# Banded attention and MLP on one core: edge and global products over all 128 rows, global attention of two pairs transposed together

## The chip, the cores and the metric

The kernel runs on one core of one Trainium2 chip. The metric is the device time of one execution in microseconds (us). For the kernel before it is 1170.29 us, the median of 3 runs (1169.29 to 1170.46). A difference of 0.2%, about 2.3 us, is what a measurement of this kernel can tell from no change.

## The reference, cut to what matters

There are 8 batches, 8 heads of 64 elements, 512 local and 32 global tokens. Global queries attend to all 544 keys; a local query attends to the 32 global keys and to local keys at most 32 positions away. The result goes through an MLP with gelu.

```python
s_g = scale * q_g @ k_all.T                 # k_all = [k_g, k_l]
out_g = softmax(s_g) @ v_all
s_ll = where(abs(i - j) <= 32, scale * q_l @ k_l.T, -1e9)
s_lg = scale * q_l @ k_g.T
out_l = softmax([s_lg, s_ll]) @ [v_g, v_l]
x = concat([out_g, out_l], axis=2)          # (4352, 512) after a reshape
out = gelu(x @ w_in) @ w_out                # 512 -> 2048 -> 512
```

## The kernel before

**Arithmetic.** All large products run in float32r. An operand is kept as a rounded part (hi) and the rest (lo), and a product is three products (hi hi, hi lo, lo hi) that are summed in PSUM. The splitting is done by ScalarE (ACT), VectorE (DVE) and GpSimd (POOL): one copies hi, another subtracts to get lo.

**Units and chunks.** Attention goes by units (batch, half of its 512 local queries, pair of heads), 64 in all. The MLP goes by chunks of 256 tokens, 16 of them and a last one for the global queries of all batches. While the MLP of one half batch is on TensorE (PE), the attention steps of the next half batch's four units stand between its products. The order of all steps comes from a table of numbers (`PRM`) and a list of due times; PE's instructions are held to this order, and the other engines' orders are made by the scheduler of the tile framework.

**A unit.** `st_s` multiplies queries and keys (tiles `s`; 12 products over 64 rows, since a head has 64 elements; the two heads of a pair lie on different rows of PE). `st_m` (DVE) adds the mask and takes the maximum, `st_e` (ACT) the exponential, `st_n` the normalization (tile `ge` holds the gathered edge columns), `st_t` transposes the result on PE (tile `t`), `st_ah` and `st_al` split it into hi and lo (tile `at`). `st_v` splits the values: `raw` (tile `vr`) comes by DMA, `vs` gets hi (copy) and lo (POOL subtraction, L530). `st_o` (L705 to L720) multiplies for one head j: four products into PSUM tile `o`. The first three run over all 128 rows. The fourth, for the edge keys of the tile next to an end of the sequence, runs over 64 rows: both heads share slot 6 of `vs`, head 0 in partitions 0 to 63 and head 1 in 64 to 127 (L713, L717). `st_c` and `st_x` add the halves of `o`.

**Global queries.** `st_sg` gives the scores of the 32 global queries (tile `sg`), gathered in `sgr`: rows are (pair, head, query), so one `sgr` holds two pairs, a group g. There are 16 groups. `gu_min`, `gu_exp`, `gu_norm` make the softmax. Then, pair by pair (i = 0, 1): `gu_t` (L783 to L791) transposes 64 rows of `sgr` in five pieces, four of 128 keys and one of the 32 global keys (tile `gt`, pool `ps_s`); `gu_a` splits into `agt`; `gu_o` (L817 to L824) multiplies in five products, the last over 32 rows (tile `go`); `gu_s`, `gu_x`, `gu_y` add the parts and transpose the result back (`gos`, `gx`, `gc`, `xg`). `agt` is one buffer, so `gu_a` of pair 1 waits until `gu_o` of pair 0 has read it.

**MLP.** `ml_h` makes h (L865 to L867), `ml_g` the gelu on ACT, `ml_l` its splitting (`gh`, and `gl` on POOL at L386), `ml_o` the second product (`acc`, L889 to L891), `ml_e` copies the result to `ob` and sends it out.

**Pools.** In PSUM, `ps_s` has two buffers for `s`, `sg`, `gt`, `go` and `gx`, and `ps_t` has two for `t` and `o`. In SBUF, the tag `vr` has two buffers for the raw values and `ob`.

**Weights.** At the start the weights come in 32 blocks as 64-bit numbers and are turned into float32 hi and lo by DVE, ACT and POOL (`w_1` to `w_4`, tiles `wraw`, `wi`, `wo`); `late_tiles` then puts `xg`, `vgs` and `agt` in their place.

Of the kernel before, what the change touches and what calls it, by code (L numbers as in the profile page):

```python
# [8 lines left out]
F32 = mybir.dt.float32  # L9
# [30 lines left out]
# Places of the steps in the order of the program, relative to their plain  # L40
# places, and (E_) the engines of steps that several engines can do.
# [282 lines left out]
def attn_mlp(ctx, tc, q_l, k_l, v_l, q_g, k_g, v_g, w_in, w_out, out):  # L324
# [29 lines left out]
    for half in range(2):  # L354
        m = cp.tile([P, WS + WF], BF16, name=f"mask{half}")
        nc.gpsimd.memset(m, 0.0)
        # (column, first key block's distance in keys from the tile's first
        # query, width) of the local key runs of the windows
# [98 lines left out]
    vs = cp.tile([P, 7, 2, D], F32R, name="vs")  # L457
# [4 lines left out]
    sgr = [cp.tile([P, R], F32, name=f"sgr{j}") for j in range(2)]  # L462
    gs = cp.tile([P, NP, P], F32R, name="gs")
# [3 lines left out]
    def late_tiles():  # L467
        # in the place of the weights' raw words
        wx.close()
        lp = ctx.enter_context(tc.tile_pool(name="lp", bufs=1))  # L470
        late["xg"] = lp.tile([P, NP, CH], F32, name="xg")
        late["vgs"] = lp.tile([P, 10, 2, D], F32R, name="vgs")
        late["agt"] = lp.tile([P, 5, 2, 2, SG], F32R, name="agt")

    # Blocks of 32 tokens x 32 elements of a pair of heads, for the transposes
    # of blocks: partitions are (head, half of the elements, token).
# [25 lines left out]
    # Values: slots are (tile 0, head 0), (tile 0, head 1), (tile 1, ...), the  # L502
    # full tile's edge rows for head 0 and 1, the simple tile's edge rows with
    # head 0 in the lower and head 1 in the upper partitions.
    def load_v(u):
        b, half, p = u
        raw = ap_.tile([P, 7, D], F32, name="vr", tag="vr", bufs=2)
# [15 lines left out]
        for r0, src, s0 in es:  # L523
            for j in range(2):
                nc.sync.dma_start(out=raw[64 * j + r0:64 * j + r0 + 32, 6, :], in_=src[j, s0:s0 + 32, :])
# [6 lines left out]
    def st_v(u):  # L532
        split_v((u,), vs, 7)

    # Exponentials and gelus stay in the order in which they are written here:
    # each change between them is a load of ScalarE's tables.
# [38 lines left out]
    def st_tg(b):  # L575
        # columns of a pair's scores for the globals: (hi, lo), head, query
# [8 lines left out]
    def windows(half):  # L585
        # (first key column, width, query tile) of the simple and the full tile
# [4 lines left out]
    # both heads at once (j = 0): the heads of a pair are on different rows of the tensor engine  # L591
# [17 lines left out]
    # columns of the simple and the full tile's windows; 224:256 stays zero  # L609
# [95 lines left out]
    def st_o(u, j):  # L705
# [7 lines left out]
        er = slice(64 * j, 64 * j + 64)  # L713
# [3 lines left out]
              (vs[er, 6], at0[er, :, 3, :], qs)]  # L717
# [4 lines left out]
    # o holds [V hi; V lo] x [A hi | A lo]  # L722
# [60 lines left out]
    def gu_t(g, i):  # L783
        # transposes of one pair's rows: [key, (head, query)]
        s = sgr[g[1]]
        r = slice(64 * i, 64 * i + 64)
# [307 lines left out]
```

## Time and profile before

| what | value |
|---|---|
| median of 3 runs | 1170.29 us |
| span of the profiled execution (first to last instruction) | 1168.5 us |
| PE busy | 1072.6 us, 92% |
| PE's weight loads (PEld) busy | 931.0 us, 80% |
| DVE busy | 775.4 us, 66% |
| ACT busy | 648.8 us, 56% |
| POOL busy | 444.2 us, 38% |
| granted PE clock, mean | 0.992 |

The profiled execution has no time of its own beside its span; the span stands 1.8 us below the median of the runs. PE's products are pipelined, so a product's duration is longer than the step from its start to the next one's start; what a product costs PE is read from such steps. A row of the timeline has the start, the time from there to the end of the row's last instruction, the engine, the line, the operation with its tiles, rows*columns of the array that it uses, partitions x elements of what it reads, and how many instructions were merged (x4). What stands in brackets is the time for which the engine sat idle before it and what ended that.

### The profile page before, as it was taken

Reading aid. Unit: us, or ns where it says so; the run is one execution under the profiler, and the core shown is the slowest. Engines: PE = TensorE matmul, PEld = TensorE weight load, DVE = VectorE, ACT = ScalarE, POOL = GpSimd, SP = SyncE. Lnnn points to the kernel's source line nnn. Section 1 sums busy time; section 2 is a strip of 40 time slices with the busy share of each in tenths; the row PEclk is TensorE's granted clock in tenths of the full one; section 3 lists DMA queues with packets and bytes.
Section 4 is the critical chain, followed back from the end, with each engine's and each line's share of the span. In section 5 each row is a group of like instructions: output and inputs, shape, how many; then the busy total and the mean of one; then the engine's idle time right before and its main releaser. Section 6 shows DMA issues by size and latency. Waiting matters only on the chain.

```text
span 1168.5 us, 21956 instructions
## 1 busy us (share of the span) xinstructions
PE 1072.6 (92%) x7104; PEld 931.0 (80%) x7104; DVE 775.4 (66%) x2281; ACT 648.8 (56%) x1566; POOL 444.2 (38%) x418
## 2 busy tenths in 40 slices
PE   0354789999999999999999999999999999999998
PEld 0234678888888888888888888888888888888996
DVE  7999997677756676567756776667656776653000
ACT  2454567456555665566656665566556655664222
POOL 5434545333433344334333433333433433343221
PEclk9999889999999999999999999999999999999999
DMA  7355423213221232123221322133212322121000
GB/s 210 99 139 137 114 72 77 41 27 77 55 64 26 64 66 57 33 55 67 63 45 41 63 53 64 21 77 61 55 30 64 65 54 41 42 49 32 1 19 19
DMA packets 283123, 71.21 MB, mean 61 GB/s; under 512 B 268417, under 2 KB 276609, under 8 KB 283009
## 3 DMA queue, kind: packets, MB, share of 16 engines
q1 hardware_dynamic: 272256, 53.04, 22.0%
q10 hardware_dynamic: 10752, 16.78, 4.7%
q8 instruction: 56, 0.92, 0.3%
q14 instruction: 59, 0.48, 0.1%
HBM read 60.82 MB, written 8.91 MB: 60 GB/s over the span
## 4 chain that ended last, share of the span: by engine, by line
PE 77%; DVE 10%; DMA 3%; issue 3%; ACT 3%; SPq 2%; POOL 1%; ACTq 0%; DVEq 0%; POOLq 0%
PE h L865 11%; PE acc L889 10%; PE h L867 10%; PE h L866 10%; PE acc L891 9%; PE acc L890 9%; PE o L719 7%; PE s L605 3%; PE go L823 2%; PE t L688 2%; DMA wraw<-in_moe_w_in_dram 2%; DVE wraw L434 1%; DVE a_t L624 1%; PE sg L747 1%; DVE wraw L433 1%
## 5 line engine op out<-in xcount | busy, mean ns | idle before, releaser
L386 POOL TENSOR_TENSOR gl<-gf,gh 128x512 fp32r<-128x512 f32 x136 | 180.5, 1327 | 360.7 <-ACT gh L379 197.3
L865 PE MATMUL h<-xh,wi 128*128 128x256 f32 x1088 | 316.6, 291 | 0.0
L866 PE MATMUL h<-xl,wi 128*128 128x256 f32 x1088 | 305.8, 281 | 0.0
L867 PE MATMUL h<-xh,wi 128*128 128x256 f32 x1088 | 305.5, 281 | 0.0
L889 PE MATMUL acc<-wo,gh 128*128 128x512 f32 x544 | 225.7, 415 | 0.4 <-DVE gh L381 0.4
L865 PEld LDWEIGHTS h<-xh,wi 128*128 128x128 f32 x1088 | 205.7, 189 | 15.3 <-issue 0.6
L891 PE MATMUL acc<-wo,gh 128*128 128x512 f32 x544 | 214.8, 395 | 0.0
L890 PE MATMUL acc<-wo,gl 128*128 128x512 f32 x544 | 212.8, 391 | 0.8 <-POOL gl L386 0.8
L866 PEld LDWEIGHTS h<-xl,wi 128*128 128x128 f32 x1088 | 206.2, 190 | 6.0
L867 PEld LDWEIGHTS h<-xh,wi 128*128 128x128 f32 x1088 | 205.9, 189 | 0.0
L540 ACT ACTIVATE gf<-h 128x512 f32<-128x512 f32 x136 | 81.4, 598 | 165.4 <-PE h L867 156.2
L530 POOL TENSOR_TENSOR vs<-vr,vs 128x448 fp32r<-128x448 f32 x64 | 75.5, 1179 | 236.2 <-DVE vs L381 133.3
L540 ACT ACTIVATE a_t<-a_t,sm 128x192 f32<-128x192 f32 (+1 forms) x256 | 116.9, 458 | 56.3 <-DVE sm L630 55.9
L540 ACT ACT_TABLE_LOAD x91 | 116.8, 1283 | 47.3 <-PE h L867 45.8
L702 DVE TENSOR_TENSOR at<-t,at 128x512 fp32r<-128x512 f32 (+1 forms) x128 | 74.8, 618 | 83.4 <-ACT at L379 83.0
L719 PE MATMUL o<-at,vs 128*128 128x256 f32 (+1 forms) x512 | 115.5, 331 | 6.9 <-DVE at L702 6.9
L891 PEld LDWEIGHTS acc<-wo,gh 128*128 128x128 f32 x544 | 102.3, 188 | 24.3
L605 PE MATMUL s<-k,q 64*128 64x192 f32 (+1 forms) x768 | 70.2, 300 | 55.2 <-ACT vs L379 27.5
L889 PEld LDWEIGHTS acc<-wo,gh 128*128 128x128 f32 x544 | 102.3, 188 | 19.5 <-DVE gh L381 0.5
L890 PEld LDWEIGHTS acc<-wo,gl 128*128 128x128 f32 x544 | 102.9, 189 | 13.5 <-POOL gl L386 1.4
L719 PEld LDWEIGHTS o<-at,vs 128*128 128x128 f32 (+1 forms) x512 | 83.0, 197 | 35.1 <-DVE at L702 7.1
L605 PEld LDWEIGHTS s<-k,q 64*128 64x128 f32 x768 | 56.2, 201 | 62.6 <-ACT vs L379 27.5
(89 smaller groups left out, 1707.1 us busy)
## 6 DMA issues: line engine op xcount, KB each, us to landing
kraw<-in_k_l_dram SPq DMA_DIRECT2D x256, 36.0 KB, 2.0
wraw<-in_moe_w_in_dram ACTq DMA_DIRECT2D x16, 512.0 KB, 4.4
wraw<-in_moe_w_out_dram ACTq DMA_DIRECT2D x16, 512.0 KB, 4.0
qraw<-in_q_l_dram SPq DMA_DIRECT2D x256, 32.0 KB, 1.9
vr<-in_v_l_dram SPq DMA_DIRECT2D x128, 64.0 KB, 2.1
vr<-in_v_l_dram SPq DMA_DIRECT2D x64, 128.0 KB, 2.4
out_dram<-ob SPq DMA_DIRECT2D x32, 256.0 KB, 2.1
vr<-in_v_g_dram SPq DMA_DIRECT2D x192, 16.0 KB, 1.9
```

What stands on the lines that cost most here:

```text
L386: (nc.vector if e == "v" else nc.gpsimd).tensor_sub(**kw)
L530: nc.gpsimd.tensor_sub(out=t[:, :n, 1, :], in0=raw[:, :n], in1=t.bitcast(F32)[:, :n, 0, :])
L540: x = nc.scalar.activation(func=func, **kw).ins
L605: nc.tensor.matmul(out=st[u, "s", jj][:, c:c + w], lhsT=qq[pr, qt * P:qt * P + P], rhs=kk[pr, k0:k0 + w], start=(i == 0 and n == 0), stop= ...
L702: nc.vector.tensor_sub(out=at[:, 1], in0=st.pop((u, "t", j))[:, :n * P].rearrange("p (n q) -> p n q", q=P), in1=at.bitcast(F32)[:, 0])
L719: nc.tensor.matmul(out=o[:, :, qsl], lhsT=l.rearrange("p s e -> p (s e)"), rhs=r, start=(n == 0), stop=(n == 3), skip_group_check=True)
L865: nc.tensor.matmul(out=h, lhsT=hi, rhs=xh[:, c], start=(c == 0), stop=False, skip_group_check=True)
L866: nc.tensor.matmul(out=h, lhsT=hi, rhs=xl[:, c], start=False, stop=False, skip_group_check=True)
L867: nc.tensor.matmul(out=h, lhsT=lo, rhs=xh[:, c], start=False, stop=(c == NCC - 1), skip_group_check=True)
L889: nc.tensor.matmul(out=acc[t], lhsT=gh[:, f % 2, tsl], rhs=hi, start=(f == 0), stop=False)
L890: nc.tensor.matmul(out=acc[t], lhsT=gl[:, f % 2, tsl], rhs=hi, start=False, stop=False)
L891: nc.tensor.matmul(out=acc[t], lhsT=gh[:, f % 2, tsl], rhs=lo, start=False, stop=(f == NF - 1))
```

## The change

**Edge products.** `vs` and `raw` get an eighth slot. Head 0's edge values go to slot 6, partitions 0 to 63, head 1's to slot 7, partitions 64 to 127. Two memsets on POOL per unit set the other halves to zero, and the split copies and subtracts 8 slots, not 7. The fourth product of `st_o` runs over all 128 rows; the rows of the other head meet zeros.

**Global keys.** The transposed weights of the 32 global keys get a tile of their own, `agg`, of 128 partitions and two pairs; it is set to zero once by two DVE copies in `late_tiles`, and only partitions 0 to 31 are written afterwards. The fifth product of `gu_o` runs over 128 rows.

**Transposes.** `gu_t` runs once per group, no longer once per pair. It transposes all 128 rows of `sgr` in five square blocks of 128, four into one `ps_s` tile and the fifth into a `ps_t` tile (`gtg`), of which 32 rows are used. `gu_a` of pair 0 also splits the global keys' part for both pairs; `gu_a` of pair 1 only its own four blocks, so that one ACT and one DVE instruction of 32 partitions fall away per group. The `ps_s` tile is held until `gu_a` of pair 1 has read it. `gu_a` of pair 1 stands right behind `gu_o` of pair 0 in the program, and `gu_x` of pair 0 behind that.

```diff
-    vs = cp.tile([P, 7, 2, D], F32R, name="vs")
+    vs = cp.tile([P, 8, 2, D], F32R, name="vs")
...
+    zero = a_ts[1][:, 0, 224:256].unsqueeze(1).unsqueeze(1).to_broadcast([P, 2, 2, 32])
...
-        late["agt"] = lp.tile([P, 5, 2, 2, SG], F32R, name="agt")
+        late["agt"] = lp.tile([P, 4, 2, 2, SG], F32R, name="agt")
+        late["agg"] = lp.tile([P, 2, 2, 2, SG], F32R, name="agg")
+        for i in range(2):
+            nc.vector.tensor_copy(out=late["agg"][:, i], in_=zero)
...
-        raw = ap_.tile([P, 7, D], F32, name="vr", tag="vr", bufs=2)
+        raw = ap_.tile([P, 8, D], F32, name="vr", tag="vr", bufs=2)
...
-                nc.sync.dma_start(out=raw[64 * j + r0:64 * j + r0 + 32, 6, :], in_=src[j, s0:s0 + 32, :])
+                nc.sync.dma_start(out=raw[64 * j + r0:64 * j + r0 + 32, 6 + j, :], in_=src[j, s0:s0 + 32, :])
...
     def st_v(u):
-        split_v((u,), vs, 7)
+        raw = st[u, "vr"]
+        nc.gpsimd.memset(raw[64:128, 6, :], 0.0)
+        nc.gpsimd.memset(raw[0:64, 7, :], 0.0)
+        split_v((u,), vs, 8)
...
-              (vs[er, 6], at0[er, :, 3, :], qs)]
+              (vs[:, 6 + j], at0[:, :, 3, :], qs)]
...
-    def gu_t(g, i):
+    def gu_t(g):
         s = sgr[g[1]]
-        r = slice(64 * i, 64 * i + 64)
-        t = ps_s.tile([P, 512], F32, name="gt", tag="s")
-        st[g, "t"] = t
+        t = ps_s.tile([P, 4, 2, 2, SG], F32, name="gt", tag="s")
+        tg = ps_t.tile([P, 512], F32, name="gtg", tag="t")
+        st[g, "t"] = t, tg
         for n in range(4):
-            nc.tensor.transpose(out=t[:, 64 * n:64 * n + 64], in_=s[r, KG[n]:KG[n] + P], identity=ident[r, r])
-        nc.tensor.transpose(out=t[0:32, 256:320], in_=s[r, 128:160], identity=ident[r, r])
+            nc.tensor.transpose(out=t[:, n], in_=s[:, KG[n]:KG[n] + P], identity=ident)
+        nc.tensor.transpose(out=tg[:, 0:P], in_=s[:, 128:128 + P], identity=ident)
...
+        a, ag = late["agt"], late["agg"]
+        t, tg = st[g, "t"]
+        src, srg = t[:, :, i], tg[0:32, 0:P].rearrange("p (i h q) -> p i h q", i=2, h=2)
+        nc.scalar.activation(out=a[:, :, :, 0, :], in_=src, func=AF.Copy)
+        if i == 0:
+            nc.scalar.activation(out=ag[0:32, :, :, 0, :], in_=srg, func=AF.Copy)
+            nc.vector.tensor_sub(out=ag[0:32, :, :, 1, :], in0=srg, in1=ag.bitcast(F32)[0:32, :, :, 0, :])
+        nc.vector.tensor_sub(out=a[:, :, :, 1, :], in0=src, in1=a.bitcast(F32)[:, :, :, 0, :])
...
     def gu_o(g, i):
-        a = late["agt"]
+        a = [late["agt"][:, n] for n in range(4)] + [late["agg"][:, i]]
...
         for n in range(5):
-            k = P if n < 4 else 32
-            nc.tensor.matmul(out=o, lhsT=a[:k, n].rearrange("p h l q -> p (h l q)"),
-                             rhs=late["vgs"][:k, 2 * n:2 * n + 2], start=(n == 0), stop=(n == 4))
+            nc.tensor.matmul(out=o, lhsT=a[n].rearrange("p h l q -> p (h l q)"),
+                             rhs=late["vgs"][:, 2 * n:2 * n + 2], start=(n == 0), stop=(n == 4))
```

The line numbers below are those of each kernel; after has a few lines more than before. On PE, the first batch's first group, where `sgr` is `sgr_150` and the products of the MLP end at L891. Before:

```order
L889 MATMUL acc_1044<-wo,gh 128x512
L890 MATMUL acc_1044<-wo,gl 128x512
L891 MATMUL acc_1044<-wo,gh 128x512
L823 MATMUL go<-vgs,agt 128x256 x5
L790 MATMUL gt<-ident,sgr_150 128x64 x4
L791 MATMUL gt<-ident,sgr_150 32x64
L719 MATMUL o<-at_1467,vs 128x2x128 x3
L719 MATMUL o<-at_1460,vs 128x2x128
L688 MATMUL t<-ident,a_t_147 128x128 x2
```

The same place after (L897 to L899 are the MLP's second product, L831 is `gu_o`, L728 is `st_o`, L698 is `st_t`):

```order
L897 MATMUL acc_1054<-wo,gh 128x512
L898 MATMUL acc_1054<-wo,gl 128x512
L899 MATMUL acc_1054<-wo,gh 128x512
L800 MATMUL gt<-ident,sgr_150 128x128 x4
L801 MATMUL gtg<-ident,sgr_150 128x128
L831 MATMUL go<-vgs,agt 128x256 x4
L831 MATMUL go<-vgs,agg 128x256
L728 MATMUL o<-at_1475,vs 128x2x128 x3
L728 MATMUL o<-at_1468,vs 128x2x128
L698 MATMUL t<-ident,a_t_147 128x128 x2
```

Pair 0's transposes, which stood some products of the MLP earlier, have moved down to where pair 1's were, and the first `go` now stands right behind them. In all later groups the transposes of both pairs stood together already, and the place stays. Before, there:

```order
L891 MATMUL acc_2798<-wo,gh 128x512
L790 MATMUL gt<-ident,sgr_150 128x64 x4
L791 MATMUL gt<-ident,sgr_150 32x64
L790 MATMUL gt<-ident,sgr_150 128x64 x4
L791 MATMUL gt<-ident,sgr_150 32x64
L865 MATMUL h<-xh,wi 128x256
```

After:

```order
L899 MATMUL acc_2813<-wo,gh 128x512
L800 MATMUL gt<-ident,sgr_150 128x128 x4
L801 MATMUL gtg<-ident,sgr_150 128x128
L873 MATMUL h<-xh,wi 128x256
L874 MATMUL h<-xl,wi 128x256
```

Ten transposes have become five, and all other products of PE stand in the order in which they stood. On POOL, in the middle of the program (`gl` is L386 in both; `ge` is L670 and L676 before, L680 and L686 after; `vs` is L530 and L537). Before:

```order
L386 TENSOR_TENSOR gl<-gf,gh 128x512
L670 TENSOR_TENSOR ge<-a_t_147,sm 128x256
L676 TENSOR_TENSOR ge<-a_t_147,sm 128x128
L386 TENSOR_TENSOR gl<-gf,gh 128x512
L530 TENSOR_TENSOR vs<-vr,vs 128x7x64
L386 TENSOR_TENSOR gl<-gf,gh 128x512
L530 TENSOR_TENSOR vs<-vr,vs 128x7x64
```

After:

```order
L386 TENSOR_TENSOR gl<-gf,gh 128x512
L680 TENSOR_TENSOR ge<-a_t_147,sm 128x256
L686 TENSOR_TENSOR ge<-a_t_147,sm 128x128
L541 MEMSET vr 64x64
L542 MEMSET vr 64x64
L541 MEMSET vr 64x64
L542 MEMSET vr 64x64
L386 TENSOR_TENSOR gl<-gf,gh 128x512
L537 TENSOR_TENSOR vs<-vr,vs 128x8x64
L386 TENSOR_TENSOR gl<-gf,gh 128x512
L537 TENSOR_TENSOR vs<-vr,vs 128x8x64
```

The memsets of two units have been placed ahead of one `gl`. Each waits for its `vr` buffer, which at this place was held by `ob` and is free when the output has been sent. DVE, ACT and SP keep their order from the second batch on, but for `gu_a`'s instructions and the places next to them; before that, while the weights are being prepared, the scheduler has exchanged many neighbours.

More of the change, by code (lines that the diff above doesn't have):

```diff
@@ L712, in st_o @@
         qf = slice(tf * P, tf * P + P)
-        er = slice(64 * j, 64 * j + 64)
         mm = [(vs[:, 2 * ts_ + j], at[:, :, 0, :], qs),
@@ L781, in gu_norm @@
         nc.vector.tensor_scalar_mul(out=s, in0=s, scalar1=ri)
-    def gu_t(g, i):
+    def gu_t(g):
         s = sgr[g[1]]
-        r = slice(64 * i, 64 * i + 64)
-        t = ps_s.tile([P, 512], F32, name="gt", tag="s")
-        st[g, "t"] = t
+        t = ps_s.tile([P, 4, 2, 2, SG], F32, name="gt", tag="s")
+        tg = ps_t.tile([P, 512], F32, name="gtg", tag="t")
+        st[g, "t"] = t, tg
         for n in range(4):
-            nc.tensor.transpose(out=t[:, 64 * n:64 * n + 64], in_=s[r, KG[n]:KG[n] + P], identity=ident[r, r])
-        nc.tensor.transpose(out=t[0:32, 256:320], in_=s[r, 128:160], identity=ident[r, r])
+            nc.tensor.transpose(out=t[:, n], in_=s[:, KG[n]:KG[n] + P], identity=ident)
+        nc.tensor.transpose(out=tg[:, 0:P], in_=s[:, 128:128 + P], identity=ident)
     def gu_a(g, i):
-        a = late["agt"]
-        t = st.pop((g, "t"))
-        for hi, pr, ks_, n in ((True, P, slice(0, 4), 4), (True, 32, slice(4, 5), 1),
-                               (False, P, slice(0, 4), 4), (False, 32, slice(4, 5), 1)):
-            src = t[:pr, 64 * ks_.start:64 * ks_.stop].rearrange("p (n h q) -> p n h q", n=n, h=2)
-            if hi:
-                nc.scalar.activation(out=a[:pr, ks_, :, 0, :], in_=src, func=AF.Copy)
-            else:
-                nc.vector.tensor_sub(out=a[:pr, ks_, :, 1, :], in0=src, in1=a.bitcast(F32)[:pr, ks_, :, 0, :])
+        a, ag = late["agt"], late["agg"]
[6 more added lines that the diff above has]
+        nc.vector.tensor_sub(out=a[:, :, :, 1, :], in0=src, in1=a.bitcast(F32)[:, :, :, 0, :])
     def gu_vl(g, i):
@@ L817, in gu_o @@
     def gu_o(g, i):
-        a = late["agt"]
+        a = [late["agt"][:, n] for n in range(4)] + [late["agg"][:, i]]
         o = ps_s.tile([P, 2, 2, D], F32, name="go", tag="s")
@@ L981, in attn_mlp @@
         at("sgc" + e, t0 + 0.4, st_sgc, u, after=[("st_sg", u)] + pv("st_sga"))
-        at("sga" + e, t0 + 0.8, st_sga, u, after=([("gu_t", (b - 1, p // 2), 1)] if b else []) + [("st_sgc", u)])
+        at("sga" + e, t0 + 0.8, st_sga, u, after=([("gu_t", (b - 1, p // 2))] if b else []) + [("st_sgc", u)])
         ex = B0 + 3.49 * STEP + DD("ex")
@@ L1009, in attn_mlp @@
             ee = str(p // 2)
+            pgu = ((b, 0) if p // 2 else (b - 1, 1)) if b or p // 2 else None
             pg = [("gu_o", (b, 0) if p // 2 else (b - 1, 1), 1)] if b or p // 2 else []
@@ L1018, in attn_mlp @@
                 at("gv" + i_, y - 2.6, gu_v, g, i, after=pg + [("late_tiles",)] + [("gu_vl", g, i)] + ([("gu_o", g, 0)] if i else []))
-                at("gt" + i_, x, gu_t, g, i, after=[("gu_norm", g)] + ([("gu_a", g, 0)] if i else []))
-                at("ga" + i_, x + 0.5, gu_a, g, i, after=pg + [("late_tiles",)] + [("gu_t", g, i)] + ([("gu_o", g, 0)] if i else []))
+                if not i:
+                    at("gt" + i_, x, gu_t, g, after=pg + [("late_tiles",), ("gu_norm", g)] + ([("gu_a", pgu, 1)] if pgu else []))
+                at("ga" + i_ if not i else "", x + 0.5 if not i else done["gu_o", g, 0] + 0.01, gu_a, g, i,
+                   after=pg + [("late_tiles",), ("gu_t", g)])
                 at("go" + i_, y, gu_o, g, i, after=[("gu_a", g, i), ("gu_v", g, i)] + ([("gu_s", g, 0)] if i else []))
                 at("gs" + i_, y + 0.6, gu_s, g, i, after=[("gu_o", g, i)] + ([("gu_x", g, 0)] if i else []))
-                at("gx" + i_, z, gu_x, g, i, after=[("gu_s", g, i)] + ([("gu_y", g, 0)] if i else []))
+                if not i:
+                    z = max(z, done["gu_o", g, 0] + 0.02 - DD("gx" + i_))
+                at("gx" + i_, z, gu_x, g, i, after=[("gu_s", g, i)] + ([("gu_y", g, 0)] if i else [("gu_o", g, 0)]))
                 at("gy" + i_, z + 0.3, gu_y, g, i, after=[("late_tiles",)] + [("gu_x", g, i)])
```

## The prediction

> **What bounds the kernel now.** I read three stretches first (columns: stretch, its length, busy us of PE, PEld, DVE, ACT and POOL with instructions, granted clock, share and GB/s of the DMA), and then what PE waited for once the weights are there.
>
> ```profile
> 0.00:150.00 150.00, 64.04 (x311) 50.18 (x311) 138.10 (x310) 68.96 (x166) 70.62 (x75) 0.97 0.54 141
> 150.00:1090.00 940.00, 935.76 (x6341) 815.74 (x6342) 635.08 (x1964) 561.51 (x1373) 356.13 (x330) 1.00 0.25 52
> ```
>
> ```profile
> PE gt L790 <- DVE sm L624: 1.4, 6, 0.4
> PE go L823 <- DVE agt L802: 1.1, 2, 0.7
> ```
>
> For 150 us DVE, busy 138 of them, turns weights into parts and PE follows. From 150 to 1090 PE is busy 936 of 940 us at full clock, and after 200 us it waits for the two things shown, 2.5 us in all. So in the middle a step taken off PE is time taken off the span, until another engine is late. The question is what the partial-row products cost PE, and who is late next. Here is one head's `st_o` between products of the MLP:
>
> ```profile
> 486.31 0.40 PE L891 MATMUL acc<-wo,gh 128*128 128x512 f32 x1
> 486.55 0.82 PE L719 MATMUL o<-at,vs 128*128 128x256 f32 x4
> 487.30 0.38 PE L865 MATMUL h<-xh,wi 128*128 128x256 f32 x1
> 487.52 0.28 PE L866 MATMUL h<-xl,wi 128*128 128x256 f32 x1
> 487.64 0.28 PE L867 MATMUL h<-xh,wi 128*128 128x256 f32 x1
> ```
>
> Between two full-row products of 256 columns the step is 0.12 us (487.52 to 487.64). From the first `o` to the second `h` are five steps, 0.59 us at that rate, and they take 0.97. The 0.38 us too much lie round the 64-row product, since the only thing that differs is its rows: it starts late, the next product starts late, and that one's follower (0.22, not 0.12) too. The 32-row product of `gu_o` does the same:
>
> ```profile
> 422.58 0.94 PE L823 MATMUL go<-vgs,agt 128*128 128x256 f32 x5
> 423.45 0.93 PE L719 MATMUL o<-at,vs 128*128 128x256 f32 x4
> ```
>
> Five steps take 0.87, not 0.59 us; the last 0.10 falls into the `o` behind it (0.93 here, 0.82 above). I take 0.38 us for it as well.
>
> **The change part by part.**
>
> *Edge products.* The counts, of the whole program and of its first 170 us:
>
> ```profile
> L719 PE MATMUL o<-at,vs 64*128 64x256 f32 x128 | 50.9, 398 | 0.0
> L719 PE MATMUL o<-at,vs 64*128 64x256 f32 x12 | 6.8, 563 | 0.0
> ```
>
> 128 - 12 = 116 lie where PE counts. By PE's order 30 of the 128 (27 of the 116) stand right ahead of the 64-row products `s`, where the change of rows comes in any case:
>
> ```profile
> 406.02 0.28 PE L867 MATMUL h<-xh,wi 128*128 128x256 f32 x1
> 406.23 0.36 PE L605 MATMUL s<-k,q 64*128 64x192 f32 x2
> 488.82 0.83 PE L719 MATMUL o<-at,vs 128*128 128x256 f32 x4
> 489.27 1.04 PE L605 MATMUL s<-k,q 64*128 64x192 f32 x12
> ```
>
> From the first `o` to `s` are 0.45 us now. After: three full steps and one into 64 rows like `h` to `s`, 3 x 0.12 + 0.21 = 0.57, less the late start of the fourth that 0.45 holds already; at worst 0.1 us lost, at best nothing. I take nothing, the cost of entering being paid once in both. The other 89 give 89 x 0.38 = 34 us.
>
> The Trainium skill's page "TensorE: Matmul & The Clock Gate" (Part 3, "What overlaps and what doesn't") speaks against this: a weight load overlaps running products only where its row group differs, which full-row products never have. These rows of the main stream say otherwise:
>
> ```profile
> L867 PE MATMUL h<-xh,wi 128*128 128x256 f32 x1088 | 305.5, 281 | 0.0
> L867 PEld LDWEIGHTS h<-xh,wi 128*128 128x128 f32 x1088 | 205.9, 189 | 0.0
> ```
>
> A load of 0.19 and a product of 0.28 us, both over 128 rows, recur every 0.12 us, so they overlap. The rule as a case is the third rival.
>
> *Global-key products.* 32 (two in each of 16 groups) x 0.38 = 12 us.
>
> *Transposes.*
>
> ```profile
> 387.19 0.39 PE L891 MATMUL acc<-wo,gh 128*128 128x512 f32 x1
> 387.42 0.38 PE L688 MATMUL t<-ident,a_t 128*128 128x128 f32 x2
> 388.30 0.28 PE L866 MATMUL h<-xl,wi 128*128 128x256 f32 x1
> 411.15 0.40 PE L891 MATMUL acc<-wo,gh 128*128 128x512 f32 x1
> 412.32 0.28 PE L866 MATMUL h<-xl,wi 128*128 128x256 f32 x1
> ```
>
> From `acc` to the second `h` pass 0.35 us without anything between (0.23 + 0.12). Seven square transposes make it 1.11, so one costs 0.11; a group's ten small ones make it 1.17, so they cost 0.82. Five square ones: 0.55, a gain of 0.27 per group, 16 x 0.27 = 4 us if nothing else holds PE.
>
> *What holds it.* The second group of each batch, on PE and DVE:
>
> ```profile
> 433.80:449.70 15.90, 15.63 (x108) 13.21 (x106) 14.95 (x49) 10.35 (x29) 5.34 (x5) 1.00 0.21 37
> 442.95 0.84 DVE L645 TENSOR_SCALAR sm<-sm 128x4 f32<-128x4 f32 x1 [0.48 <-ACT a_t L540]
> 444.42 0.46 PE L790 MATMUL gt<-ident,sgr 64*128 64x64 f32 x4 [0.19 <-DVE sm L624]
> 449.14 0.54 DVE L802 TENSOR_TENSOR agt<-gt,agt 128x256 fp32r<-128x256 f32 x2
> 449.82 1.02 PE L823 MATMUL go<-vgs,agt 128*128 128x256 f32 x5
> ```
>
> DVE is busy 14.95 of 15.9 us up to `go`, and `go` starts 0.14 us after DVE's last `agt`. DVE can come forward by little more than its wait of 0.48, less about 0.09 that the wider copy of `vs` takes (below). PE would have come earlier by the 0.76 of two edge products and the 0.27 of the transposes. So 0.65 of 1.03 us are lost, and PE waits openly for `agt`. In each batch's first group DVE has a wait of 1.63 us ahead:
>
> ```profile
> 410.26 0.17 DVE L645 TENSOR_SCALAR sm<-sm 128x4 f32<-128x4 f32 x1 [1.63 <-ACT a_t L540]
> ```
>
> The edge products' gain fits there, but the transposes' 0.27 comes behind that wait and is lost. Seven batches x (0.65 + 0.27) = 6 us.
>
> *First batch.* `go` now stands right behind the transposes. How long their splitting takes, from rows of this place:
>
> ```profile
> 174.96 0.46 PE L790 MATMUL gt<-ident,sgr 64*128 64x64 f32 x4
> 175.50 0.48 ACT L800 ACTIVATE agt<-gt 128x256 fp32r<-128x256 f32 x2 [0.17 <-PE gt L791]
> 176.02 0.54 DVE L802 TENSOR_TENSOR agt<-gt,agt 128x256 fp32r<-128x256 f32 x2 [0.19 <-ACT agt L800]
> ```
>
> 1.6 us from `gt` to the end of `agt`, of which the transposes cover a third; with a shorter wait for `gx` behind it, 2 us once (1 to 5, as DVE is full there).
>
> *The other engines.*
>
> ```profile
> L530 POOL TENSOR_TENSOR vs<-vr,vs 128x448 fp32r<-128x448 f32 x64 | 75.5, 1179 | 236.2 <-DVE vs L381 133.3 <-DMA vr<-in_v_l_dram 55.7 <-DMA kraw<-in_k_l_dram 14.6
> L381 DVE CAST vs<-vr 128x448 fp32r<-128x448 f32 x56 | 34.5, 616 | 28.9 <-PE o L719 8.9 <-DMA kgr<-in_k_g_dram 8.5 <-DMA vr<-in_v_g_dram 6.9
> masks.py:197 POOL MEMSET ident<- 128x128 f32 x1 | 0.2, 204 | 0.3 <-POOLq L1078 0.3
> L386 POOL TENSOR_TENSOR gl<-gf,gh 128x512 fp32r<-128x512 f32 x136 | 180.5, 1327 | 360.7 <-ACT gh L379 197.3 <-issue 50.8 <-PE t L691 45.7
> ```
>
> Eight slots for seven: 1179/7 = 0.17 us more on POOL and 616/7 = 0.09 on DVE per unit, 11 and 5 us in all. 128 memsets, at most 0.2 us each (that one is four times as large), 26 us. POOL stays below half busy; ahead of `gl` it is idle 361 us, 2.7 per instruction, into which four memsets of 0.8 us at most fit. I take nothing; without that cover it would be 0.8 us at each of 16 places, 13 us.
>
> *The start.* DVE gets two zero copies more, about 0.4 us each, and many neighbours change places. I take nothing, with 6 us to either side: DVE's idle time there is 12 us, and half of it is my choice.
>
> *Sum.* 34 + 12 + 4 - 6 - 2 = 42 us off the span of 1168.5: 1126.5, and with the 1.8 us by which the median stands above it 1128. If PE kept all of it and its present waits went too (0.65 + 0.27 a batch back, and about 0.7 of waits round `gt` and `go`, seven times), and 2 us came off the start, it would be 1128 - 6 - 5 - 2 = 1115.
>
> **The rivals.**
>
> *DVE is late everywhere.* If the shorter pair of `o` ahead of `s` uncovered DVE or ACT in every unit, as in the second groups, the 0.76 us of 29 such pairs (58 of the 89 products) would go: 22 us back, less 3 counted already: 1147. For it: DVE at 68% in the middle would come near 71%. Against: it waits 1.63 us for ACT in the one group. Chance 0.14.
>
> *POOL holds the MLP up: slower.* Two of the memsets wait for the sending of `ob`, with `gl` behind them on POOL and `acc` behind `gl`.
>
> ```profile
> DMA to landing us min/median/max: 1.6/2.0/4.1
> ```
>
> This decides if PE loses more than 42/16 = 2.6 us at each of 16 chunks. If a landing of 4.1 us and 0.8 us of memsets were wholly uncovered, PE would lose 16 x 4.9 = 78 us: 1206. Against it: the 2.7 us of mean idle time ahead of `gl`, and the landing begins long before. Chance 0.04.
>
> *Full-row loads don't overlap: slower.* By the rule cited above each changed product would cost load plus product, 0.19 + 0.28 = 0.47, and so would the one behind it: 0.94 in place of 0.24 + 0.38. That is 0.32 x (89 + 32) = 39 us more: 1209. The step of 0.12 speaks against it. Chance 0.02.
>
> *The rows aren't the cause.* If the late steps came from the slot or the PSUM columns, they would stay, and only the waits would be added: about 1172. Chance 0.02.
>
> **How the numbers follow.** The forecast, 1128, has 0.78. The range reaches from 1114, where PE keeps nearly everything, to 1148, which takes in the first rival and half of the loss of the start; the ends beyond it and the last three rivals are the 2 in 10 left out. Faster by over 0.2% (2.3 us, about what a measurement tells from no change): 0.78 + 0.14 = 0.92; within it 0.03, the last rival and a little; slower 0.05.
>
> **What would show it.** Right: no row of 64 or 32 rows at `o` and `go`; one `o` of four products and the next two `h` in steps of 0.12; five transposes per group in 0.55 us; PE waiting 5 to 15 us for `agt` and little else. Wrong: the late steps still there; PE waiting for `gl`, `vs` or `q`; the stretch up to the MLP's steady run longer than 156 us.

## The result, and the profile after

The changed kernel takes 1141.55 us (median of 4 runs, 1140.44 to 1142.11), the kernel before 1170.13 (4 runs, 1169.29 to 1170.46): a ratio of 0.975, with a 95% interval of 0.974 to 0.977. So 28.6 us went, where 42 were forecast. The profiled execution spans 1138.6 us, 29.9 less than before.

The first thing to look at is the place that the prediction costed, one head's `st_o` between products of the MLP, on PE after the change (columns: start, us, engine, line, operation, tile, shapes, count):

```profile
479.59 0.40 PE L899 MATMUL acc<-wo,gh 128*128 128x512 f32 x1
479.82 0.63 PE L728 MATMUL o<-at,vs 128*128 128x256 f32 x4
480.29 0.28 PE L873 MATMUL h<-xh,wi 128*128 128x256 f32 x1
480.41 0.28 PE L874 MATMUL h<-xl,wi 128*128 128x256 f32 x1
```

From the first `o` to the second `h` are now 0.59 us (479.82 to 480.41), five steps of 0.12, where it was 0.97. The five `go` of one pair with the `o` behind them, and the joint transposes:

```profile
419.07 0.64 PE L831 MATMUL go<-vgs,agt 128*128 128x256 f32 x4
419.54 0.28 PE L831 MATMUL go<-vgs,agg 128*128 128x256 f32 x1
419.66 0.64 PE L728 MATMUL o<-at,vs 128*128 128x256 f32 x4
...
408.10 0.39 PE L899 MATMUL acc<-wo,gh 128*128 128x512 f32 x1
408.33 0.60 PE L800 MATMUL gt<-ident,sgr 128*128 128x128 f32 x4
408.77 0.27 PE L801 MATMUL gtg<-ident,sgr 128*128 128x128 f32 x1
408.80 0.36 PE L873 MATMUL h<-xh,wi 128*128 128x256 f32 x1
409.00 0.28 PE L874 MATMUL h<-xl,wi 128*128 128x256 f32 x1
```

Five `go` steps take 0.59 us (419.07 to 419.66), where they took 0.87. From `acc` (408.10) to the second `h` (409.00) pass 0.90, so the five transposes cost 0.90 - 0.35 = 0.55. The unit prices are as forecast, so the loss is elsewhere. PE's busy time by stretch (columns as in the prediction), and its waits after 200 us, show a part of it:

```profile
0.00:150.00 150.00, 60.21 (x309) 49.35 (x309) 135.54 (x307) 67.71 (x162) 74.31 (x88) 0.97 0.53 139
150.00:1062.00 912.00, 894.42 (x6272) 804.63 (x6273) 642.32 (x1953) 562.33 (x1361) 380.46 (x446) 0.99 0.26 54
```

```profile
PE go L831 <- DVE agt L811: 6.9, 10, 1.4
PE h L874 <- DVE xl L386: 1.2, 1, 1.2
PE t L698 <- DVE xs L743: 0.8, 1, 0.8
PE sg L756 <- DVE sm L634: 0.8, 2, 0.6
```

From 150 us on PE is idle for 17.6 us (912.00 - 894.42), against 4.2 before, and DVE is busy for 70% of the stretch instead of 68%. The named waits grew from 2.5 to 9.7 us, most of it at `go`. They understate the loss: a product that starts late while the one ahead of it still runs leaves no idle time, and shows only in the steps from start to start.

The other piece lies at the start. The first product of the second chunk of the MLP (the same product of the program in both), before and after:

```profile
191.08 0.39 PE L865 MATMUL h<-xh,wi 128*128 128x256 f32 x1
```

```profile
196.14 0.36 PE L873 MATMUL h<-xh,wi 128*128 128x256 f32 x1
```

The changed kernel is 5.1 us behind at this product, and 29.9 ahead at the end. So it gains 35 us from here on. In the middle, from the chunk that begins at 379.01 us before to the one four batches on at 880.43, a batch takes 125.4 us; after, 376.74 to 857.68, it takes 120.2. That is 5.1 us of gain in each batch.

### The profile page after: what moved, and what is told of

Its sections match the earlier page's. It is cut to its first block, busy times and chain, and to the rows that moved or that the text cites. A ratio compares the mean times of both kernels' runs of the same rounds, so it can differ in the third digit from the quotient of the medians.

```text
span 1138.6 us, 21902 instructions
## 1 busy us (share of the span) xinstructions
PE 1025.6 (90%) x7024; PEld 917.4 (81%) x7024; DVE 780.1 (69%) x2267; ACT 647.2 (57%) x1550; POOL 471.7 (41%) x546
## 4 chain that ended last, share of the span: by engine, by line
PE 59%; DVE 17%; DMA 9%; ACT 6%; issue 4%; SPq 4%; POOL 1%; DVEq 0%; ACTq 0%; POOLq 0%
PE acc L897 8%; PE h L874 8%; PE h L875 8%; PE h L873 8%; PE acc L898 7%; PE acc L899 7%; PE o L728 4%; PE s L615 3%; DVE a_t L634 2%; DMA kraw<-in_k_l_dram 2%; ACT a_t L550 2%; PE t L698 2%; PE go L831 2%; DMA vr<-in_v_l_dram 2%; ACT L550 2%
## 5 line engine op out<-in xcount | busy, mean ns | idle before, releaser
L873 PE MATMUL h<-xh,wi 128*128 128x256 f32 x1088 | 309.9, 285 | 0.0
L875 PE MATMUL h<-xh,wi 128*128 128x256 f32 x1088 | 305.6, 281 | 0.0
L386 POOL TENSOR_TENSOR gl<-gf,gh 128x512 fp32r<-128x512 f32 x136 | 180.0, 1324 | 290.7 <-ACT gh L379 145.6
L897 PE MATMUL acc<-wo,gh 128*128 128x512 f32 x544 | 224.9, 413 | 0.8 <-DVE gh L381 0.8
L899 PE MATMUL acc<-wo,gh 128*128 128x512 f32 x544 | 215.2, 396 | 0.0
L537 POOL TENSOR_TENSOR vs<-vr,vs 128x512 fp32r<-128x512 f32 x64 | 84.2, 1315 | 230.0 <-DVE vs L381 102.1
L899 PEld LDWEIGHTS acc<-wo,gh 128*128 128x128 f32 x544 | 102.6, 189 | 24.0
L615 PE MATMUL s<-k,q 64*128 64x192 f32 (+1 forms) x768 | 67.5, 304 | 56.3 <-ACT vs L379 27.7
L897 PEld LDWEIGHTS acc<-wo,gh 128*128 128x128 f32 x544 | 102.9, 189 | 18.7 <-DVE gh L381 1.0
L615 PEld LDWEIGHTS s<-k,q 64*128 64x128 f32 x768 | 53.5, 201 | 67.5 <-ACT vs L379 27.7
L728 PE MATMUL o<-at,vs 128*128 128x256 f32 x512 | 82.1, 296 | 10.3 <-DVE at L712 10.1
L728 PEld LDWEIGHTS o<-at,vs 128*128 128x128 f32 x512 | 73.4, 201 | 14.1 <-DVE at L712 10.2
```

Of the source, the lines that this page charges most:

```text
L386: (nc.vector if e == "v" else nc.gpsimd).tensor_sub(**kw)
L537: nc.gpsimd.tensor_sub(out=t[:, :n, 1, :], in0=raw[:, :n], in1=t.bitcast(F32)[:, :n, 0, :])
L615: nc.tensor.matmul(out=st[u, "s", jj][:, c:c + w], lhsT=qq[pr, qt * P:qt * P + P], rhs=kk[pr, k0:k0 + w], start=(i == 0 and n == 0), stop= ...
L728: nc.tensor.matmul(out=o[:, :, qsl], lhsT=l.rearrange("p s e -> p (s e)"), rhs=r, start=(n == 0), stop=(n == 3), skip_group_check=True)
L873: nc.tensor.matmul(out=h, lhsT=hi, rhs=xh[:, c], start=(c == 0), stop=False, skip_group_check=True)
L875: nc.tensor.matmul(out=h, lhsT=lo, rhs=xh[:, c], start=False, stop=(c == NCC - 1), skip_group_check=True)
```

## The experiments

**Theory**, after the result: each change between full- and part-row products costs PE 0.38 us, as forecast, and the 13 us that are missing went into the start and into waits for VectorE. **Rival**: the padding (128 memsets, eight slots to split) eats them. A second question is whether it is the change of rows at all, or something else of these products.

### One part alone

`edge_only` takes the edge part of the diff (slots, memsets, loads, `mm`) and leaves the global part as before. `edge_no_pad` is the kernel before with the full-row product over the old slot 6, where each head also meets the other head's edge values, so that its result is changed:

```
-              (vs[er, 6], at0[er, :, 3, :], qs)]
+              (vs[:, 6], at0[:, :, 3, :], qs)]
```

`global_only` is the changed kernel with slots, memsets, loads and this product as before.

> Only the edge products of the change (64 rows to 128, slots 6 and 7, 128 memsets, the wider loads and splits); the global-key part stays as before. Theory (each product on part of the rows between products on all rows costs TensorE about 0.38 us, and what is missing of the forecast went into the start and into waits for VectorE at the global queries): 89 x 0.38 = 34 us less, less 2 to 4 us at the start, nothing lost at the global queries, so 1138 to 1142 us, as fast as the whole change. Rival (the padding work on GpSimd and VectorE costs the 13 us that are missing): 1147 to 1152 us.

> The kernel before with one edit: the fourth product of each head takes all 128 rows of the old slot 6, where both heads' edge values lie, so that each head also gets the other head's edge term (that part of the result is changed); no eighth slot, no memsets, loads and splits as before. Theory: the time of edge_only less up to 3 us for the start, 1136 to 1140 us. Rival (padding costs the missing 13 us): 10 to 13 us below edge_only, and 1133 to 1137 us or less.

> Only the global-key part of the change (joint transposes, fifth product over all rows, the zeroed tile); the edge products stay on 64 rows with seven slots. Theory: 32 x 0.38 + 4 = 16 us less on TensorE, of which 6 to 13 us go back into waits for VectorE before the global queries' products and into the start: 1160 to 1167 us. Rival (padding of the edges costs the missing 13 us, the global part gives what it should): 1154 to 1157 us.

Measured: `edge_only` 1148.96 us (ratio to before 0.982, 0.981 to 0.984), 21 us less; `edge_no_pad` 1148.14 (0.981, 0.980 to 0.983); `global_only` 1157.41 (0.989, 0.988 to 0.991), 12.6 less. Padding is not where the gain went: without it the edge part is 0.8 us faster, with overlapping intervals, and not 10 to 13. But the theory's numbers failed too. `edge_only` (1138 to 1142 expected) lies where the rival had put it, `edge_no_pad` (1136 to 1140) 8 us above its range, and `global_only` just below the 1160 to 1167 of the theory, nearest to the rival's 1154 to 1157. The theory had said that the edge part loses nothing at the global queries, and there it fails: these are PE's longest waits after 200 us in `edge_only`, a kernel in which the code of the global queries is untouched.

```profile
PE go L826 <- DVE agt L805: 5.0, 10, 1.1
PE h L869 <- DVE xl L386: 1.2, 1, 1.2
```

So these waits don't need the new global code; PE is earlier by the edge products, and meets them. They are also not the largest loss. To find all of it, cut PE's program into blocks: a block is a run of products of the attention between two products of the MLP (`go5 t7` is five `go` and then seven `t`), and its cost is the time from the product before it to the second product behind it, less the MLP's own steps of 0.118 (`h`) and 0.232 us (`acc`). From the second chunk on, the cheapest passages of all blocks together fall by 33.9 us in `edge_only`, as the theory had it (89 x 0.38 = 34). What the blocks cost beyond their cheapest passages rises by 2.5: 4.8 more at the blocks `go5` and `go5 t7`, but 4.3 less at the transposes `gt`, which had waited before. The MLP's own steps lose 7.0, 3.5 of it at products of `h` that wait for VectorE's `xl` and 1.7 at products of `acc` that wait for GpSimd's `gl`, each with the step behind. And 3.0 are lost at the start. That leaves the 21.3 by which the span fell.

The two parts alone give 21 + 12.6 = 33.6 us, together 28.6. By the same accounts, the two parts alone lose 2.4 us in the blocks, and together 6.9; at the start they lose 3.8 alone and 5.1 together; in the MLP's own steps it is 8.2 alone and 5.9 together. Waits at the global queries are what grows most, which fits two gains that draw on the same slack of VectorE; that reading was not tried by itself.

### Is it the change of rows?

If so, two part-row products side by side should share one price. `edge_adjacent` is the kernel before with

```
+        if j:
+            mm = mm[3:] + mm[:3]
```

so that head 1's 64-row product comes first, behind head 0's last one.

> The kernel before with one line: head 1 takes its 64-row product first, so that where the two heads' products stand behind each other (about 29 to 35 of 64 units) both 64-row products lie side by side between full-row ones. Same products, same rows, same loads. Theory (the price is of the change of rows, not of the product): 29 to 35 x 0.38 = 11 to 13 us less, 1157 to 1159 us. Rival (the price is of each 64-row product itself, its rows or its weight load): 1170 us, no change.

Measured: 1170.70 us (1.0007, 0.9998 to 1.0016). No change, the rival's number. Its trace, however, shows two effects that cancel: PE's blocks of eight `o` went from 1.96 to 1.47 us, and those of four `o` ahead of the 64-row `s` went from 1.52 to 1.91. The theory should have said this beforehand. In most of the even units the old order put head 1's 64-row product right ahead of `s`, and the edit took it away from there. Two kernels part the effects, with `if j and u[2] % 2 == 1` (odd units, whose heads stand side by side) and `== 0` (even units, most of which stand ahead of `s`):

> The kernel before, with head 1's 64-row product put first in the odd units alone, whose two heads' products stand directly behind each other; the even units keep it last, where the 64-row score products follow it. Theory (the price is of the change of rows): the blocks with eight products fell from 1.961 to 1.466 us in edge_adjacent, so 25 to 28 x 0.495 = 12 to 14 us less, of which up to 2 go to waits for VectorE: 1156 to 1160 us. Rival (edge_adjacent did nothing because no such price exists): 1170 us.

> The kernel before, with head 1's 64-row product put first in the even units alone, so that it no longer stands ahead of the 64-row score products but between two full-row products. Theory: those blocks rose from 1.516 to 1.911 us in edge_adjacent, so 26 to 28 x 0.395 = 10 to 11 us more, 1179 to 1182 us. Rival (no price of the change of rows): 1170 us.

Measured: `adj_odd` 1162.12 us (0.993, 0.992 to 0.994), 7.8 less; `adj_even` 1178.53 (1.007, 1.006 to 1.009), 8.6 more. The block of eight in the kernel before and in `adj_odd`:

```profile
498.10 0.40 PE L891 MATMUL acc<-wo,gh 128*128 128x512 f32 x1
498.33 0.40 PE L747 MATMUL sg<-k,gs 128*128 128x256 f32 x2
498.57 1.68 PE L719 MATMUL o<-at,vs 128*128 128x256 f32 x8
500.18 0.39 PE L865 MATMUL h<-xh,wi 128*128 128x256 f32 x1
```

```profile
496.58 0.40 PE L893 MATMUL acc<-wo,gh 128*128 128x512 f32 x1
496.81 0.40 PE L749 MATMUL sg<-k,gs 128*128 128x256 f32 x2
497.06 1.39 PE L721 MATMUL o<-at,vs 128*128 128x256 f32 x8
498.28 0.28 PE L867 MATMUL h<-xh,wi 128*128 128x256 f32 x1
```

The same eight products, six of 128 and two of 64 rows, last 1.61 us up to the first `h` (498.57 to 500.18) when the part-row ones stand apart, and 1.22 when they are neighbours (497.06 to 498.28); with the late steps behind, the block is 0.49 cheaper. That is more than one price of 0.38, and the starts say why: the two neighbours, on the two halves of the rows, start 3 ns apart, so the second also saves its own step of 0.12. In `adj_even`, four `o` that start with the 64-row product (the row has the shape of its first product) take 0.87 us up to `s`, where they took 0.45 with that product last, and their block is 0.39 dearer:

```profile
490.51 0.94 PE L721 MATMUL o<-at,vs 64*128 64x256 f32 x4
491.38 0.93 PE L605 MATMUL s<-k,q 64*128 64x192 f32 x12
```

Neighbours that overlap would be cheaper even if each 64-row product had its own price, so one more reading is needed. The twelve `s` of the kernel before, all on 64 rows, come in pairs that start 3 ns apart, and from pair to pair pass 0.11 us. Only at the edges of the twelve are steps late: 0.21 into the first pair and 0.19 to the second, 0.20 to the first `acc` and 0.34 to the next (0.23 otherwise). The block costs 1.05 us in all, six steps of 0.11 and one price of 0.38 for twelve products. So the price is of the change of rows and not of the product. The Trainium skill says as much ("TensorEngine Tiling (Array Packing)", section "Key Properties": changing the tiling mode, not just the tile, drains TensorE); the traces agree, and give 0.38 us for going to part of the rows and back.

`adj_odd` came out above its forecast (1156 to 1160). Its blocks' cheapest passages fell by 14.4 us, a little more than the 12 to 14 of the theory. Of these, 1.6 are lost up to the second chunk, 2.1 in longer waits in the blocks (those for `agt` after 200 us come to 6.4) and 3.8 in late steps of the MLP, at `xl` and `gl` again. `adj_even` came out 0.5 us below its forecast (1179 to 1182).

### The start

VectorE is busy for 135.5 of the first 150 us, and the changed kernel puts two copies into its queue that zero `agg`, behind a wait (a stretch of VectorE after the change):

```profile
164.09 0.43 DVE L381 CAST wo<-wraw 128x512 fp32r<-128x512 f32 x1
165.94 0.37 DVE L478 CAST agg<-a_t 128x128 fp32r<-128x128 f32 x2 [1.42 <-POOL wo L450]
166.22 0.42 DVE L381 CAST gh<-gf 128x512 fp32r<-128x512 f32 x1
```

`agg` lies where the raw weights lay, so its zeroing waits for GpSimd's last read of them, and `gh` and all behind it wait along. `agg_pool` gives these copies to GpSimd, where they follow that read anyway:

```
-            nc.vector.tensor_copy(out=late["agg"][:, i], in_=zero)
+            nc.gpsimd.tensor_copy(out=late["agg"][:, i], in_=zero)
```

> The changed kernel, with the two copies that zero the new tile made by GpSimd instead of VectorE; there they stand behind the same GpSimd instruction for which VectorE waited. Theory (part of the missing 13 us is in the start, which VectorE sets): 1.4 us of wait and 2 x 0.37 us of copies leave VectorE's queue, 1139 to 1140 us. Rival (the start is set by the padding or by the first global group): within 0.7 us of the changed kernel, 1141 to 1142 us.

`all_no_pad` is `agg_pool` with the edge products of `edge_no_pad`.

> agg_pool, with the edge products over all 128 rows of the old single slot 6 (each head also gets the other head's edge term, so that part of the result is changed): no eighth slot, no memsets. Theory (the padding costs next to nothing): 1 to 3 us below agg_pool, 1135 to 1137 us, and what there is of it lies in the first 200 us. Rival (the padding eats the gain that is missing): 1125 to 1129 us.

Measured: `agg_pool` 1138.24 us (0.973, 0.971 to 0.974), 3.3 below the changed kernel, 0.8 under the theory's range and the fastest of the kernels here that leave nothing out; `all_no_pad` 1136.07 (0.971, 0.970 to 0.973), 2.2 below that. Both rivals fail here: the start is not set by the padding alone, and the padding does not eat the missing gain. (The theory of `agg_pool` counted the copies twice: the 0.37 us of the row are for both, so that with the wait of 1.42 they account for 1.8 us of VectorE's time.) Where the first product of the second MLP chunk starts in each:

| kernel | start, us | against before |
|---|---|---|
| before | 191.08 | |
| global_only | 191.86 | +0.8 |
| edge_no_pad | 191.01 | -0.1 |
| edge_only | 194.11 | +3.0 |
| changed | 196.14 | +5.1 |
| agg_pool | 193.33 | +2.3 |
| all_no_pad | 190.93 | -0.1 |

So the 5.1 us of the start go away in two steps: 2.8 with the zero copies, 2.4 with the padding. The medians say the same (3.3 and 2.2). The two don't simply add: the padding alone costs 3.0, the copies and all of the global part with the old edges 0.8. Why 0.37 us of copies and two memsets per unit cost so much is seen one step further on, at PE's first `o` behind them, before and after, each with a stretch of 2.5 us that follows:

```profile
170.92 0.93 PE L719 MATMUL o<-at,vs 128*128 128x256 f32 x4 [0.89 <-DVE at L702]
176.00:178.50 2.50, 2.50 (x22) 2.37 (x22) 1.63 (x6) 1.97 (x6) 2.34 (x2) 1.00 0.23 39
```

```profile
174.15 0.74 PE L728 MATMUL o<-at,vs 128*128 128x256 f32 x4 [3.30 <-DVE at L712]
176.00:178.50 2.50, 2.50 (x7) 1.81 (x7) 1.94 (x11) 0.00 (x0) 0.00 (x0) 0.50 0.10 20
```

PE starts this `o` 3.2 us later, having waited 3.30 us for VectorE and not 0.89; in `agg_pool`, without the copies, it starts at 171.34, which is the whole 2.8. (The 1.8 us of wait and copies are the most of that; the other 1.0 is not accounted for.) And 1.5 us after the `o` starts, the granted clock (third column from the right) falls from 1.00 to 0.50, for some 3.4 us, in which a step of `acc` takes 0.43 us and not 0.23. At half the clock that is 1.7 us of work lost, an estimate from these figures; with the 3.2 it is nearly all of the 5.1. The same stretch of half clock, behind the same `o`, stands in `agg_pool` (wait 1.93 us), `edge_only` (2.78), `adj_odd` (2.39), `go_later` (3.31) and `k2_pool` (2.00). It is missing in the kernel before and seven others, whose waits there are 0.98 to 2.20 us. So the longest waits had it and the shortest had not; what decides in between, no run here shows. By the same estimate it is 1.7 of the 2.4 us that the padding costs in `agg_pool`, and all of `adj_odd`'s 1.6.

### The waits in the middle

Four kernels try to win back the waits at `go`. `go_later` moves two numbers of the table in the changed kernel, `go_gx_later` (on `agg_pool`) one of these and the transpose behind it; `gt_early` (on `agg_pool`) moves the joint transposes; `k2_pool` (on `agg_pool`) moves a subtraction of VectorE's to GpSimd:

```
go_later     'go00' -4.0197 -> -2.2697   'go10' -0.7737 -> 0.9763
go_gx_later  'go10' -0.7737 -> 0.9763    'gx10' -0.3424 -> 1.4076
gt_early     'gt00' -2.8301 -> -6.3301   'gt10' -3.4669 -> -6.9669
k2_pool      'E_k21' 'v' -> 'p'
```

> The changed kernel, with the first global-query product of each group placed half a step of the MLP later (two numbers of the table). Theory (the rest of the missing us are waits of these products for VectorE's agt, some 10 us in the blocks go5 and go5 t7 by start-to-start times, against 3 in the kernel before): most of that goes, 1133 to 1138 us. Rival (VectorE itself is late, so the wait moves to the next product that needs it): 1140 to 1143 us.

> agg_pool, with the first global-query product of the second groups and the transpose behind it both half a step of the MLP later, so that twelve products of the MLP stand between the two (in go_later none stood there in these groups, and gx waited 11.9 us for gos). Theory (these products come before VectorE has made agt, and half a step covers it): the waits of the blocks go5, 6.0 us in agg_pool, go, and gx keeps its distance: 1132 to 1135 us. Rival (VectorE itself is late by then, so the next product that needs it waits instead): 1137 to 1140 us.

> agg_pool, with the joint transposes of each group one step of the MLP earlier (two numbers of the table; the softmax ahead of them is done about 18 us before they start). The copies and subtractions that make agt then stand some eight places earlier in VectorE's queue and three earlier in ScalarE's, ahead of the next unit's normalization and of the transposes of its keys; the products themselves stay where they are. Theory (these products wait because agt stands late in the queues, about 11 us in the blocks go5 and go5 t7 of agg_pool): half to all of it goes, 1128 to 1133 us. Rival (VectorE as a whole is behind, so what is made earlier makes something else later): 1136 to 1139 us.

> agg_pool, with the subtraction that makes the low part of the keys (128x320, one in each unit, 56 of 64 units) on GpSimd instead of VectorE. On VectorE it took 0.48 us where GpSimd stood idle as it began and 0.87 us on average, up to 1.6, where GpSimd was busy, and it stands ahead of agt in VectorE's queue. Theory (the waits of the global-query products are VectorE's lateness): some 45 us leave VectorE, half or more of the 11 us in the blocks go5 and go5 t7 go, and the score products don't wait, 1129 to 1135 us. Rival (GpSimd's own queue, with its splits and the padding, becomes the bound of the score products or of gl): 1139 to 1150 us.

Measured: `go_later` 1147.34 us (0.981, 0.980 to 0.982), `go_gx_later` 1143.41 (0.978, 0.976 to 0.979), `gt_early` 1176.92 (1.005, 1.004 to 1.007), `k2_pool` 1153.43 (0.985, 0.984 to 0.986). All four are slower than the kernel they start from. PE's waits after 200 us, of `go_later` and `go_gx_later`:

```profile
PE gx L844 <- DVE gos L839: 11.9, 8, 1.7
PE go L831 <- DVE agt L811: 3.7, 4, 1.6
```

```profile
PE go L831 <- DVE agt L811: 4.2, 4, 1.6
PE acc L897 <- ACT ob L379: 3.1, 4, 1.3
PE go L831 <- POOL vgs L537: 2.9, 5, 0.8
```

In `go_later` the second groups' `go` came to stand next to its own `gx`, which now waits for the sum in between. In `go_gx_later` that is mended, and the next in line appear: some `acc` wait for ScalarE's copy to `ob`, and the second `go` of a group waits for `vgs`, a single buffer that is refilled only when the first `go` has read it. With the steps behind, `ob` costs 4.4 us, the largest new loss. In `gt_early` the products of `go` wait no more, but this does:

```profile
PE gt L800 <- DVE sm L634: 30.4, 13, 2.5
PE sg L756 <- DVE sm L634: 1.3, 2, 0.7
```

Moved right behind `s`, `gt` asks for a PSUM buffer of the tag that `s` uses before VectorE has read the scores out of it. The blocks `go5` and `go5 t7` fell to 0.59 and 1.35 us, their prices without a wait, so the theory's mechanism holds (they wait because `agt` stands late in the queues), and its number fails (1128 to 1133), since a dearer wait took its place. That wait costs more than its length. One of the 13, at 318 us, with the granted clock in the wait, behind it and after that:

```profile
316.00:318.00 2.00, 0.00 (x0) 0.00 (x0) 1.92 (x11) 2.00 (x8) 0.64 (x1) 1.00 0.42 69
320.00:321.00 1.00, 1.00 (x7) 1.00 (x6) 1.00 (x3) 0.24 (x1) 1.00 (x2) 0.50 0.00 0
322.00:324.00 2.00, 2.00 (x14) 1.78 (x13) 1.93 (x10) 1.09 (x6) 0.00 (x0) 1.00 0.30 48
```

Behind 12 of these 13 waits, of 2.3 to 2.5 us each, up to a dozen steps of `h` take 0.21 us and not 0.12; the MLP's own steps lose 13 us more than in `agg_pool`, a third of what this kernel is slower. In `k2_pool` VectorE's own waits tell:

```profile
DVE at L712 <- ACT at L379: 75.0, 37, 3.2
DVE qt L571 <- POOL k L386: 49.0, 45, 2.3
```

The transposed queries use the buffer of the transposed keys, so VectorE now stands still for 49 us until GpSimd has done the subtraction. On PE the loss shows in the MLP's own steps, 12.8 us over those of `agg_pool`: those that wait for VectorE's `xl` and `xh` cost 10.5 (3.0 there), those that wait for `gl` 6.2 (1.7 there). In all four the rival had the direction, and each came out slower than even its range. VectorE's work was moved and no slack was found in the order as it is. The waits at `go` stand at the end of a chain PE, ScalarE, VectorE, PE, and each cure ran into another wait, three of the four at a buffer that is shared.

## Why the forecast was right in direction and too high by 12 us

The 12 us are counted by the spans of the profiled executions, 42 forecast and 29.9 measured; by the medians they are 13.

1. **What bounds it.** Right: in the middle a step off PE is time off the span, until VectorE is late.
2. **Edge products, 89 x 0.38.** Right. The single blocks of four `o` fell by 0.386 us, those of eight by 0.75. For the 27 ahead of `s`, taken at nothing, the blocks went from 1.516 to 1.523. That the price is of the change of rows is shown by `adj_odd`, `adj_even` and the twelve `s`.
3. **Global-key products and transposes, 12 + 4.** Right: 0.28 at the five steps of `go` and 0.10 at the `o` behind it, 0.55 per group of transposes. The cheapest passage of each block, summed over the 232 blocks from the second chunk on, gives 241.3 us before and 193.5 after: 47.8 less. The forecast has 50, of which 2.1 (two edge products, two of `go`, two groups of transposes) lie before that chunk.
4. **What holds it, 6 us.** This term was too small: it stops at the global queries. The same blocks cost 9.4 us more than their cheapest passages before and 16.3 after, 6.9 more. That is near the 6 forecast, but partly by luck: the blocks `go5` and `go5 t7` rose by 7.1, `t7 gx1` by 2.3, the pairs of `sg` by 1.5, and 5.0 of waits at `gt`, which the prediction priced only in its upper bound, went away. What the term left out is that PE, once earlier, meets other chains in each half batch. The MLP's own steps went from 2.2 us under the nominal 0.118 and 0.232 us a step to 3.7 over it, 5.9 us of late steps for which nothing was forecast: 2.8 more where `h` waits for VectorE's `xl` (0.15 us at a time, once 1.34, and 0.11 in the step behind) and 1.7 where `acc` waits for GpSimd's `gl` (387.38 to 387.80 for a step of 0.23, and 0.10 in the step behind). The rest, 1.4 us, is in delays of at most 0.11 us each and stays open. 47.8 - 6.9 - 5.9 is 35.0, as the landmarks have it.
5. **First batch, 2 us.** Right in size: its block of `gt`, `go`, `o`, `t` and `gx` took 4.29 us, 2.1 above the sum of its parts. But a stretch of half clock lies over the beginning of it.
6. **The other engines, nothing.** Right after the start, wrong in it. The memsets take 0.15 us each, 19 in all, and GpSimd has room; but edges with padding reach the second chunk 3 us later than edges without, 1.7 of it by the stretch of half clock.
7. **The start, nothing, 6 us to either side.** The second term that failed: 5.1 us late, within the bounds given. Both causes stood in the prediction, unpriced. The copies were counted at 0.4 us each and take 0.37 together; what they cost was their place in VectorE's queue, behind a wait of 1.42 us for GpSimd. That PE's longer wait for VectorE would be followed by half the clock was in no term.

So the 12 us between the forecast 42 and the 29.9 of the span are 5.1 at the start and 7.0 behind it (42.0 forecast from the second chunk on, 35.0 measured): 5.9 at the MLP's own steps and 0.9 at the blocks, the rest rounding. The measured 1141.55 lies within the range of 1114 to 1148, but nearer to the first rival's 1147 than to 1128; it is inside because the range took in that rival and half of the loss of the start.

The rivals: VectorE late everywhere (1147) described the right engine in the wrong place, since the blocks of eight `o`, where it put the loss, kept all of their gain in the median (1.96 to 1.21 us). GpSimd, past the start, did not hold up the MLP by more than 0.2 us at a time. Full-row loads that don't overlap would have made each `o` step 0.47 us; the trace has 0.12. And the rows were the cause.

## What to carry to other kernels

A lone product on part of the rows costs by where it stands, so put such products next to each other, or next to others that use part of the rows, before padding them; but an order that helps one neighbour can take the product away from another. When one engine bounds a kernel at 99%, price a saving on it by the slack of every chain that feeds it, not of the nearest one alone: here a quarter of the gain went into waits for VectorE and GpSimd, and moving one of them by a table only found the next. And price an instruction in a full queue by what it waits for and what waits behind it, not by how long it runs: 0.37 us of zeroing cost 2.8.

## What the runs showed of the hardware that was not expected

VectorE's subtraction for the keys has one shape throughout, and yet its mean rose from 714 to 830 ns (the row in the kernel before, then after):

```profile
L386 DVE TENSOR_TENSOR k<-kt,k 128x320 fp32r<-128x320 f32 x64 | 45.7, 714 | 6.4 <-ACT k L379 6.2
```

```profile
L386 DVE TENSOR_TENSOR k<-kt,k 128x320 fp32r<-128x320 f32 x64 | 53.1, 830 | 6.1 <-ACT k L379 5.9
```

After 200 us, it took 0.48 us in the mean where GpSimd was idle as it began (16 times before, 13 after), and where GpSimd was busy 0.78 before (37 times) and 0.93 after (40 times). One of them in `agg_pool`, on VectorE and on GpSimd:

```profile
557.06 1.60 DVE L386 TENSOR_TENSOR k<-kt,k 128x320 fp32r<-128x320 f32 x1
...
557.03 1.28 POOL L386 TENSOR_TENSOR gl<-gf,gh 128x512 fp32r<-128x512 f32 x1
```

It began 0.03 us behind GpSimd's `gl` and ended 0.35 us after it. After the change, all 29 that began in the first 0.92 us of `gl` ended 0.35 us behind it, wherever in it they began; alone, such a subtraction takes 0.48. The Trainium skill has a rule for this ("SBUF — State Buffer", section "SBUF: two separate sides"): a VectorE operation with two SBUF inputs and a GpSimd operation that reads SBUF share a port pair as an exclusive lock, and the later one blocks for the whole of the other. The trace agrees in the main (of the 0.48 only 0.35 come behind `gl`), and shows how it looks: as a longer busy time of VectorE and not as a wait. Over 64 units that is 7.4 us of VectorE's time which the change did not ask for by a single instruction of its own. How much of the waits at `go` comes from it was not tried separately. It does not decide the time by itself: in `all_no_pad`, the fastest of these kernels, the subtraction takes 875 ns in the mean, more than after the change.

The second is the granted clock. Behind 12 of 13 waits of 2.3 to 2.5 us in `gt_early`, and behind the wait for the first `o` in six of fourteen kernels (1.93 to 3.31 us), it stood at 0.50 for some 3 us, so that a wait cost PE up to 1.7 us beyond its own length (the estimate above).
